# Attention scores by three fp32r passes instead of fp32, with a block diagonal for the leftover queries, in a fused attention and two-MLP kernel

## The chip, the cores and the metric

One core of a Trainium2 chip. The metric is device time in microseconds of one execution, lower is better.

## What is computed

Attention over 4 batches and 8 heads, 576 positions, head size 64, then two MLPs (512 to 2048 to 512) over the 2304 tokens, all to float32 accuracy. The part of the reference that matters:

```python
scores = scale * np.matmul(q, k.transpose(0, 1, 3, 2))        # scale = 1/8
thresh = np.max(scores, axis=-1, keepdims=True) - tau
scores = np.where(scores >= thresh, scores, -1000000000.0)
scores = scores - np.max(scores, axis=-1, keepdims=True)
attn = np.exp(scores)
attn = attn / (np.sum(attn, axis=-1, keepdims=True) + 1e-09)
return np.matmul(attn, v).astype(np.float32)
...
h = x @ w_in
g = np.maximum(h, 0.0) + alpha * np.minimum(h, 0.0)           # the second MLP: g = h - np.tanh(h)
return (g @ w_out).astype(np.float32)
```

The MLP weights come as float64.

## The kernel before, in words

Two heads stand side by side on the 128 partitions, head `h` on rows 0 to 63 and head `h + 1` on rows 64 to 127. A unit `u` is a pair of heads in one batch and one query block; there are 32. Block `qb = 0` has queries 0 to 255, `qb = 1` has 256 to 511 and brings the last 64 queries along as leftover. A unit is worked on in two visits of 128 queries (64 visits), and a unit with `qb = 1` in one leftover visit more (16). Two units of a batch in a row can have the same heads; then the second keeps the keys and values of the first (`brings`).

A visit (`attend`, L639) does: scores on TensorE in plain fp32 (L649), per head and per chunk of 320 and 256 keys, each head on its own row half, into the PSUM tiles `sc0` and `sc1`; the row maximum on VectorE (L523); threshold (L526); a steep Prelu on ScalarE that leaves zero above the threshold and something very low under it (helper L289); Exp with its sum (L533); then the softmax is scaled and turned. Units 0 to 3 (`WHOLE = 4`) turn it with TensorE (L551, L554) and multiply with plain fp32 values (L674, L677). The others split it into two fp16 parts in a buffer of the tag `rw` (L571 and its ScalarE copy at L284, L575, then a small copy at L286 or L284) and turn it with a transposing DMA (L585) into a tile `eT`; values are split into three bf16 parts (L502) and multiplied in 46 matmuls (L637). The result goes as a high and a low fp32r part into `x0`, `x1` (L284, L691), the input of the first MLP. The leftover visit (`attend_left`, L706) does the same for 64 queries of both heads at once: its scores are four 64x64 tiles (L715).

An MLP in fp32r takes three passes: high by high, high by low, low by high. The first products stand on L782 (12 matmuls of 256 columns per 128 features), the second ones of the first MLP on L969, those of the second MLP on L891 and L898. The first MLP has nine blocks of tokens; block 2b + qb needs the four units of that batch and query block, the ninth needs all leftovers. The second MLP starts after the last product of attention, block by block as the first MLP's blocks are stored. All weights are brought from float64 into two fp32r parts by ScalarE, VectorE and GpSimd (`turned_float`, L321, and `piece`).

Queries and keys have buffers of their own (tags `q` and `ks`, two each). Both are loaded by SP (L476, L484), and ScalarE multiplies the queries by 1/8 in place (L284, from L479).

The order of the work on every engine is laid out ahead by a planner (`Plan.order`, L114). Each operation has a cost for each engine that may do it, a rank, reads, writes, and the buffers it takes. The planner keeps a clock for each engine and always issues the operation that can start first, the lower rank winning among equals. Where several engines may do an operation, the one with the lowest start plus a penalty gets it (`POOL_PEN`, `ACT_PEN`, `DVE_PEN`). The ranks come from `TA` (per visit), `PA` and `PB` (weights), `MLP_PE`, `MLP_G`, `PREP` and the table `OFF`; the buffer counts from `BUFS`. TensorE fills its waits at the start with 220 small matmuls (`warm`, L1016). SP issues every DMA, and does so in order.

Of the kernel before, what the change touches and what calls it, by code (L numbers as in the profile page):

```python
# [52 lines left out]
POOL_PEN = 0.8491  # L53
ACT_PEN = 0.7974
# [6 lines left out]
XR = -5886.5085  # L61
# [3 lines left out]
DVE_PEN = 0.7259  # L65
OFF = {"S": -1656.89, "M": -1361.12, "TH": -2264.05, "E": -795.89, "X": -1209.11, "R": -3863.73, "N": -3770.75, "NL": -1862.72, "F": -1987.79, "DT": 37.37, "T": 495.28, "H": -576.12, "AV": -1213.3, "XC": -519.32, "XH": 818.59}
# [3 lines left out]
    "q": 2, "ks": 2, "vs": 4, "v3": 3, "e": 3, "st": 2, "eT": 3, "rw": 4, "raw0": 2, "raw1": 3, "tw": 2,  # L70
# [161 lines left out]
def attention_mlp_mlp(ctx: ExitStack, tc: tile.TileContext, kv, q0, q1, tau, w1i, w1o, alpha, w2i, w2o, out):  # L232
# [23 lines left out]
    none = cpool.tile([P, P], F32, name="none")  # L256
    ident = tpool.tile([P, P], F32, name="ident")
# [200 lines left out]
    brings_v = [brings[u] if u != WHOLE else u for u in range(NV // 2)]  # L458
# [6 lines left out]
    def prep(u, rank):  # L465
        b, qb, h = visits[2 * u]
        k = brings[u]
        q, ks = ("q", u), ("ks", k)
        width = BLK + D * qb
        rate = P * 4 / DMA_RATE  # L470


        def load_q(e):
            x = take(tpool, q, [P, BLK + D], F32, "q", BUFS["q"])
# [6 lines left out]
        def load_k(e):  # L481
            x = take(tpool, ks, [P, S], F32, "ks", BUFS["ks"])
            for a in range(2):
                e.dma_start(out=x[HALVES[a]], in_=kv[b, h + a][HALVES[a], :S])  # L484

        add({"SYNC": max(1.1, rate * width)}, rank - 6, load_q, [ROOM], [q], takes=[("q", q)], lag=DMA_LAG)
        if k == u:
            add({"SYNC": max(1.1, rate * S)}, rank - 6, load_k, [ROOM], [ks], takes=[("ks", ks)], lag=DMA_LAG)
        add({"ACT": 0.45}, rank, scale, [("const", 0), ROOM], [q])
        k = brings_v[u]  # L490
# [21 lines left out]
    def softmax(tile, n, slots, rank, eT, alone=False, w=False):  # L512
# [125 lines left out]

    def attend(v, rank):  # L639
# [6 lines left out]
        def scores(e, heads):  # L646
            for c in CHUNKS:
                for a in heads:
                    e.matmul(  # L649
                        sc[slots[a]][:, 192:192 + S][:, c], lhsT=T["q", u][HALVES[a], j * P:(j + 1) * P], rhs=T["ks", k][HALVES[a], c],  # L650
                        start=True, stop=True,
                    )

        alone = v < SOLO
        for heads in ((0,), (1,)) if alone else ((0, 1),):
            add({"PE": 1.3}, rank + OFF["S"], lambda e, heads=heads: scores(e, heads), [("ks", k), ("q", u), ROOM], [("sc", slots[a], "s") for a in heads],
# [5 lines left out]
    def attended(u, rank):  # L662
        b, qb, h = visits[2 * u]
        k, w = brings_v[u], one(u)
# [16 lines left out]
        add({"PE": 2.3 if w else 2.7}, rank + OFF["AV"], products, [*reads, *with_v(k, w), ROOM], [pk, ("products", u)], bank)  # L681
# [323 lines left out]
    def clear(e):  # L1005
        e.memset(none, 0.0)
        make_identity(nc, ident)
# [127 lines left out]
```

## Time and profile before

| | |
|---|---|
| median of 3 runs | 1083.64 us (1081.25 to 1085.19) |
| profiled execution, its own time | 1083.33 us |
| its span, first to last instruction | 1081.5 us |
| TensorE busy | 1058.8 us, 98% |
| VectorE busy | 768.2 us, 71% |
| ScalarE busy | 569.5 us, 53% |
| GpSimd busy | 124.1 us, 11% |

The span is the time from the first to the last recorded instruction; the execution's own time holds a little more. Busy time of TensorE counts a matmul from its start to its modelled end, and matmuls overlap, so busy is not the same as working at full rate. In the rows, PE is TensorE's matmuls, PEld its weight loads, DVE is VectorE, ACT ScalarE, POOL GpSimd and SP the engine that issues DMAs.

### The profile page before, as it was taken

The page shows a single profiled execution, that of the slowest core. Times are in us where ns is not written, and L with a number is a line of the kernel's source. Part 1 is how long each engine was busy: PE and PEld are TensorE (multiplying, and loading weights), DVE is VectorE, ACT ScalarE, POOL GpSimd, SP SyncE. Part 2 cuts the span into 40 slices and gives each one's busy share as a digit, 9 for nine tenths or more (in the row PEclk, how much of TensorE's full clock was granted, in tenths as well). Part 3 has the DMA queues.
Part 4 walks back from the last instruction along what each step waited for, and adds up shares of the span by engine and source line. Part 5 has one row for each costly group of instructions (what it writes and reads, how often), then busy time and mean ns, then how long its engine had stood idle before and what let it go on. Part 6 is the DMA issues. An engine that isn't in the chain of part 4 may idle for free.

```text
span 1081.5 us, 23833 instructions
## 1 busy us (share of the span) xinstructions
PE 1058.8 (98%) x9594; PEld 979.0 (91%) x9594; DVE 768.2 (71%) x1638; ACT 569.5 (53%) x1135; POOL 124.1 (11%) x142
## 2 busy tenths in 40 slices
PE   9979999999999999999999999999999999999997
PEld 7658888888898888888899999999999999999997
DVE  6998978768778778777764558985656656556554
ACT  5777876766677677776642337642223322232322
POOL 2432211101111002120100001000000000000000
PEclk9989999999999999999999999999999999999999
DMA  8557987767566676756471315501101001010000
GB/s 228 178 156 185 226 172 127 142 112 145 110 148 135 111 148 144 147 126 132 84 214 44 118 58 197 177 25 35 41 1 40 19 21 40 2 40 21 1 21 20
DMA packets 189998, 110.55 MB, mean 102 GB/s; under 512 B 160704, under 2 KB 172224, under 8 KB 189888
## 3 DMA queue, kind: packets, MB, share of 16 engines
q1 hardware_dynamic: 189888, 109.03, 43.1%
q8 instruction: 75, 1.23, 0.5%
q14 instruction: 35, 0.29, 0.1%
HBM read 61.28 MB, written 9.96 MB: 66 GB/s over the span
## 4 chain that ended last, share of the span: by engine, by line
PE 53%; DVE 1%; ACT 0%; issue 0%; DVEq 0%; ACTq 0%
PE hp L782 17%; PE sc L891 13%; PE pt L782 10%; PE acc L969 8%; PE sc L898 5%; PE pt L637 1%; PE sc L649 0%; PE sc L715 0%; ACT e L289 0%; DVE rw L575 0%; DVE st L523 0%; DVE o L924 0%; ACT e L533 0%; DVE rw L571 0%; DVE st L526 0%
## 5 line engine op out<-in xcount | busy, mean ns | idle before, releaser
L782 PE MATMUL hp<-x,ihi 128*128 128x256 f32 x1728 | 323.8, 287 | 4.4 <-DVE st L539 2.2
L782 PEld LDWEIGHTS hp<-x,ihi 128*128 128x128 f32 x1728 | 270.4, 193 | 17.5 <-issue 10.7
L782 PE MATMUL hp<-x,ilo 128*128 128x256 f32 x864 | 245.2, 284 | 0.0
L969 PE MATMUL acc<-g,ohi 128*128 128x256 f32 x1152 | 215.7, 287 | 0.0
L969 PEld LDWEIGHTS acc<-g,ohi 128*128 128x128 f32 x1152 | 179.3, 192 | 10.0 <-issue 9.4
L782 PEld LDWEIGHTS hp<-x,ilo 128*128 128x128 f32 x864 | 166.7, 193 | 0.0
L969 PE MATMUL acc<-g,olo 128*128 128x256 f32 x576 | 162.9, 283 | 0.0
L891 PE MATMUL sc<-wp,g 128*128 128x256 f32 x1134 | 144.9, 283 | 0.0
L891 PEld LDWEIGHTS sc<-wp,g 128*128 128x128 f32 x1134 | 140.0, 192 | 0.0
L289 ACT ACTIVATE e<-sc,st 128x576 f32<-128x576 f32 x144 | 101.8, 737 | 26.4 <-DVE st L526 25.5
L533 ACT ACTIVATE e<-e,natau 128x576 f32<-128x576 f32 x144 | 110.5, 771 | 0.4
L523 DVE TENSOR_REDUCE st<-sc 128x1 f32<-128x576 f32 x144 | 105.2, 747 | 7.6 <-PE sc L715 6.8
L969 PEld LDWEIGHTS acc<-g,olo 128*128 128x128 f32 x576 | 110.5, 192 | 0.0
L803 DVE SCALAR_TENSOR_TENSOR mr<-mr,nalpha,hp 128x256 f32<-128x256 f32 x144 | 63.5, 475 | 62.2 <-ACT mr L796 62.1
L575 DVE SCALAR_TENSOR_TENSOR rw<-e,st,rw 128x576 f16<-128x576 f32 x128 | 104.2, 840 | 2.9 <-ACT rw L284 2.5
L782 PE MATMUL pt<-x,ihi 128*128 128x256 f32 x576 | 105.2, 283 | 0.0
L782 PEld LDWEIGHTS pt<-x,ihi 128*128 128x128 f32 x576 | 90.9, 192 | 1.3
L292 DVE TENSOR_TENSOR g<-mr,g 128x512 fp32r<-128x512 f32 (+1 forms) x134 | 85.7, 639 | 5.0 <-ACT g L284 3.6
L649 PE MATMUL sc<-ks,q 64*128 64x320 f32 (+1 forms) x512 | 82.3, 433 | 1.1 <-ACT e L289 0.7
L796 ACT ACTIVATE mr<-hp 128x512 f32<-128x512 f32 x72 | 42.7, 593 | 76.0 <-PE hp L782 73.4
L782 PE MATMUL pt<-x,ilo 128*128 128x256 f32 x288 | 81.5, 283 | 0.0
L637 PE MATMUL pt<-eT,vs 128*64 128x256 f16 (+1 forms) x1584 | 74.3, 246 | 3.8 <-DMA eT<-rw 3.6
(103 smaller groups left out, 1398.4 us busy)
## 6 DMA issues: line engine op xcount, KB each, us to landing
vs<-in_kv_dram SPq DMA_DIRECT2D x58, 160.0 KB, 2.9
rw<-in_w1i_dram SPq DMA_DIRECT2D x16, 512.0 KB, 5.5
rw<-in_w1o_dram SPq DMA_DIRECT2D x16, 512.0 KB, 4.8
rw<-in_w2i_dram SPq DMA_DIRECT2D x16, 512.0 KB, 4.7
rw<-in_w2o_dram SPq DMA_DIRECT2D x16, 512.0 KB, 4.2
ks<-in_kv_dram SPq DMA_DIRECT2D x56, 144.0 KB, 3.1
x1d<-o SPq DMA_DIRECT2D x18, 256.0 KB, 2.6
rw<-x1d SPq DMA_DIRECT2D x9, 512.0 KB, 3.7
```

Source lines behind the costliest of these rows:

```text
L289: e.activation(out=out_, in_=in_, func=AF.Prelu, alpha=alpha, **kw)
L292: e.tensor_tensor(out=out_, in0=in_, in1=hi.bitcast(F32), op=ALU.subtract)
L523: e.tensor_reduce(out=T[st][:, 0, j:j + 1], in_=x(s), axis=AX.X, op=ALU.max, negate=True)
L533: e.activation(out=w_, in_=w_, func=AF.Exp, bias=natau, scale=1.0, accum_out=T[st][:, 2, j:j + 1])
L575: e.scalar_tensor_tensor(out=x_[:, S + D:], in0=w_, scalar=r, in1=x_[:, :S], op0=ALU.mult, op1=ALU.subtract)
L637: e.matmul(po[HALVES[a]], lhsT=plane((k, a), part, c), rhs=eT(a, block), start=(i == 0), stop=(i == len(TERMS) - 1), skip_group_check=True)
L649: e.matmul(sc[slots[a]][:, 192:192 + S][:, c], lhsT=T["q", u][HALVES[a], j * P:(j + 1) * P], rhs=T["ks", k][HALVES[a], c], start=True, sto ...
L782: e.matmul(hq[:, k, :], lhsT=weight(l, "i", part, f // 4)[:, c, (f % 4) * P:(f % 4 + 1) * P], rhs=T[f"x{x}", m][:, c, :], start=(n0 + n == ...
L803: e.scalar_tensor_tensor(out=T[r][:, k, :], in0=T[r][:, k, :], scalar=nalpha[:, f0 + k:f0 + k + 1], in1=hq[:, k, :], op0=ALU.mult, op1=ALU ...
L891: e.matmul(out_, lhsT=x[:, a], rhs=y[:, b], start=(n == 0 and i == 0 and number in (1, 2, 5, 4)), stop=(n == NPAIR - 1 and i == 2), skip_g ...
L898: e.matmul(two_banks(3 - 2 * t), lhsT=x, rhs=y, start=False, stop=(n == NPAIR - 1 and k == 1 and i == 2), skip_group_check=True)
L969: e.matmul(acc[t][:, (c % 2) * BLK:(c % 2 + 1) * BLK], lhsT=w[:, c * P:(c + 1) * P], rhs=g[:, k, :], start=(f == 0 and n == 0 and c % 2 == ...
```

## The change

From unit 4 on (`NATIVE = 4`) queries and keys are split into a high fp32r part and a low one, and the scores are the sum of three fp32r passes: high by high, low by high, high by low. Queries and keys are loaded into one tile of the tag `rw` (four buffers, shared with the fp16 parts and with the raw weights), and the parts go to the tags `qh` and `kh`, two buffers each. The high part is a copy on ScalarE, VectorE or GpSimd, the low part a subtraction on VectorE or GpSimd. The leftover queries of both heads go into a 128x128 block diagonal `last`, cleared once at the start, so that the leftover scores are six matmuls over all 128 rows. Units 0 to 3 keep plain fp32 scores, read from the raw tile. Queries are no longer scaled: the 1/8 goes into the threshold and into Prelu. Unit 4 now brings keys of its own. `vs` goes from four buffers to three, `eT` from three to two. The planner's constants and some of its costs are new.

```diff
-TA = 3.0306
-PA, PB = 1607.411, 3.1322
-MLP_PE = 1522.9469
-MLP_G = -1792.0778
-PREP = 2618.4454
-WHOLE, SOLO = 4, 0
+TA = 19.6723
+PA, PB = 2239.503, 0.1787
+MLP_PE = 139.5993
+MLP_G = -1579.1484
+PREP = 2168.8771
+WHOLE, SOLO, NATIVE = 4, 0, 4
...
-    "q": 2, "ks": 2, "vs": 4, "v3": 3, "e": 3, "st": 2, "eT": 3, "rw": 4, "raw0": 2, "raw1": 3, "tw": 2,
+    "qk": 2, "qh": 2, "kh": 2, "vs": 3, "v3": 3, "e": 3, "st": 2, "eT": 2, "rw": 4, "raw0": 2, "raw1": 3, "tw": 2,
...
-        same = u and visits[2 * u][::2] == visits[2 * u - 1][::2]
+        same = u and u != WHOLE and visits[2 * u][::2] == visits[2 * u - 1][::2]
...
+        parts = [("qh", BLK, 0, BLK)] + ([("kh", S, BLK + D, S)] if k == u else [])
...
+        def load_qk(e):
+            x = take(apool, raw, [P, 1024], F32, "rw", BUFS["rw"])
             for a in range(2):
                 e.dma_start(out=x[HALVES[a], :width], in_=packed_q[qb][b, h + a][HALVES[a]])
-        def scale(e):
-            copy(e, T[q][:, :width], T[q][:, :width], scale=qscale)
+            for a in range(2) if k == u else ():
+                e.dma_start(out=x[HALVES[a], BLK + D:BLK + D + S], in_=kv[b, h + a][HALVES[a], :S])
+        def hi(e, name, size, at, n):
+            copy(e, take(tpool, (name, u), [P, 2, size], F32R, name, BUFS[name])[:, 0, :n], T[raw][:, at:at + n])
+        def lo(e, name, at, n):
+            sub(e, T[name, u][:, 1, :n], T[raw][:, at:at + n], T[name, u][:, 0, :n])
+        def left_hi(e, a):
+            copy(e, last[HALVES[a], 0, HALVES[a]], T[raw][HALVES[a], BLK:BLK + D])
+        def left_lo(e, a):
+            sub(e, last[HALVES[a], 1, HALVES[a]], T[raw][HALVES[a], BLK:BLK + D], last[HALVES[a], 0, HALVES[a]])
...
+        for x in parts if u >= NATIVE else ():
+            name, size, at, n = x
+            y = (name, u)
+            add(any_of(0.1 + n * 0.00082, 0.07 + n * 0.00052, 0.09 + n * 0.001), rank + OFF["KS"], lambda e, x=x: hi(e, *x), [raw, ROOM], [(*y, 0)], takes=[(name, y)])
+            add(either(0.065 + n * 0.00105, 0.1 + n * 0.00232), rank + OFF["KS"], lambda e, x=x: lo(e, x[0], *x[2:]), [raw, (*y, 0), ROOM], [(*y, 1)])
...
-            e.tensor_scalar(out=T[st][:, 1, a:b], in0=T[st][:, 0, a:b], scalar1=1.0, scalar2=atau, op0=ALU.mult, op1=ALU.add)
+            e.tensor_scalar(out=T[st][:, 1, a:b], in0=T[st][:, 0, a:b], scalar1=qscale, scalar2=atau, op0=ALU.mult, op1=ALU.add)
...
-            prelu(e, take(tpool, ("e", (tile, j)), [P, S], F32, "e", BUFS["e"]), x(s), STEEP, bias=T[st][:, 1, j:j + 1], scale=1.0)
+            prelu(e, take(tpool, ("e", (tile, j)), [P, S], F32, "e", BUFS["e"]), x(s), STEEP, bias=T[st][:, 1, j:j + 1], scale=qscale)
...
+    def multiply_last(e, u, to):
+        kh, kl = (T["kh", brings[u]][:, part] for part in range(2))
+        for c in CHUNKS:
+            for i, (part, y) in enumerate(((0, kh), (1, kh), (0, kl))):
+                e.matmul(to[:, c], lhsT=last[:, part], rhs=y[:, c], start=(i == 0), stop=(i == 2))
+
+    def multiply(e, u, to, s, heads):
+        if u < NATIVE:
+            terms = [(T["qk", u], T["qk", brings[u]][:, BLK + D:])]
+        else:
+            (qh, ql), (kh, kl) = ([x[:, part] for part in range(2)] for x in (T["qh", u], T["kh", brings[u]]))
+            terms = [(qh, kh), (ql, kh), (qh, kl)]
+        for c in CHUNKS:
+            for i, (x, y) in enumerate(terms):
+                for a in heads:
+                    e.matmul(to(a, c), lhsT=x[HALVES[a], s], rhs=y[HALVES[a], c], start=(i == 0), stop=(i == len(terms) - 1))
```

The rest of the diff is the wiring of these, the new values of `OFF` and of the penalties, and costs such as 2.8 for 2.7 (a unit's product) or 0.72 for 0.705 (four products of the MLP).

## Rows read from the trace of the kernel before

**Rows 1.** The span and the mean granted clock of the core.

```profile
core 0: 1081.5 us, clock 0.995
```

**Rows 2.** Busy us (instructions) by stage: PE, PEld, DVE, ACT, POOL; clock, DMA, GB/s.

```profile
60.00:100.00 40.00, 33.60 (x290) 27.66 (x291) 36.48 (x74) 29.42 (x63) 11.03 (x12) 0.87 0.63 152
...
100.00:547.00 447.00, 441.22 (x4601) 390.80 (x4601) 351.61 (x759) 314.50 (x678) 68.09 (x87) 1.00 0.70 140
547.00:690.00 143.00, 143.00 (x1256) 142.83 (x1255) 94.63 (x190) 60.80 (x105) 4.93 (x4) 1.00 0.43 134
690.00:1081.50 391.50, 385.89 (x3019) 376.49 (x3017) 237.37 (x510) 121.87 (x210) 17.50 (x7) 1.00 0.08 27
```

**Rows 3.** Waits of TensorE's matmuls, 100 to 547 us: total, times, longest; the first line.

```profile
PE pt L637 <- DMA eT<-rw: 3.6, 6, 0.9
```

**Rows 4.** The chain that ended last: start, us, what; one of many alike.

```profile
556.13 2.88 PE hp L782 x24
```

**Rows 5.** Timeline of TensorE around one score visit: start us, us, instruction, count.

```profile
299.37 0.28 PE L782 MATMUL hp<-x,ilo 128*128 128x256 f32 x1
299.58 1.24 PE L649 MATMUL sc<-ks,q 64*128 64x320 f32 x8
300.75 0.51 PE L782 MATMUL hp<-x,ihi 128*128 128x256 f32 x2
301.10 0.28 PE L782 MATMUL hp<-x,ilo 128*128 128x256 f32 x1
```

**Rows 6.** The instructions of line 649: ns min/median/max, first and last start.

```profile
L649 PE MATMUL sc<-ks,q x512: 376/429/899, 11.4 to 533.2; 64*128 64x320 f32 x86, 64*128 64x256 f32 x85
```

**Rows 7.** Timeline of TensorE at the start of the second MLP.

```profile
693.85 2.91 PE L898 MATMUL sc<-wp,g 128*128 128x512 f32 x12
696.60 0.40 PE L782 MATMUL pt<-x,ihi 128*128 128x256 f32 x2
```

**Rows 8.** Timeline of TensorE around one leftover visit.

```profile
220.53 1.19 PE L715 MATMUL sc<-ks,q 64*64 64x320 f32 x8
...
221.98 0.27 PE L782 MATMUL hp<-x,ilo 128*128 128x256 f32 x1
```

**Rows 9.** Groups by line and shape: busy us, mean ns; and line 284's scaling of queries.

```profile
L286 DVE TENSOR_SCALAR wp<-tw 128x256 fp32r<-128x256 f32 x1 | 0.3, 286 | 0.0
...
L286 DVE TENSOR_SCALAR g<-mr 128x512 fp32r<-128x512 f32 x57 | 24.5, 430 | 1.6
...
L292 DVE TENSOR_TENSOR wp<-tw,wp 128x256 fp32r<-128x256 f32 x6 | 2.5, 419 | 0.3 <-ACT wp L284 0.3
...
L292 DVE TENSOR_TENSOR g<-mr,g 128x512 fp32r<-128x512 f32 x80 | 55.6, 695 | 4.9 <-ACT g L284 3.6
...
L286 DVE TENSOR_SCALAR eT<-hp 64x128 f32<-64x128 f32 x15 | 4.2, 279 | 0.2
...
L284 ACT ACTIVATE q<-q,qscale x32: 491/534/577, 10.6 to 507.0; 128x256 f32<-128x256 f32 x16, 128x320 f32<-128x320 f32 x16
```

**Rows 10.** The tile eT's instructions and landings; then groups by line and shape.

```profile
L637 PE MATMUL pt<-eT,vs x1584: 189/272/300, 87.6 to 550.5; 128*64 128x256 f16 x133, 128*64 128x64 f16 x65
...
L585 SPq DMA_TRANSPOSE eT<-rw x128: 1242/1314/2477, 70.5 to 545.2; - x128
...
DMA to landing us min/median/max: 3.2/3.4/5.9
...
L637 PE MATMUL pt<-eT,vs 128*64 128x256 f16 x1008 | 62.1, 274 | 3.7 <-DMA eT<-rw 3.6
...
L637 PE MATMUL pt<-eT,vs 128*64 128x64 f16 x576 | 12.2, 197 | 0.0
...
L284 ACT ACTIVATE rw<-e,st 128x576 f16<-128x576 f32 x71 | 54.2, 773 | 31.7 <-DVE st L539 12.2 <-issue 7.1 <-ACT e L533 3.5
...
L575 DVE SCALAR_TENSOR_TENSOR rw<-e,st,rw 128x576 f16<-128x576 f32 x128 | 104.2, 840 | 2.9 <-ACT rw L284 2.5
...
L284 ACT ACTIVATE rw<-rw 128x64 f16<-128x64 f16 x102 | 25.3, 253 | 43.3 <-DVE rw L575 41.5 <-DMA q<-in_q_dram 1.1 <-DMA ks<-in_kv_dram 0.4
```

More of the change, by code (lines that the diff above doesn't have):

```diff
@@ L481, in load_k @@
[L481 to L489, printed above, removed]
@@ L491, in prep @@
+        for a in range(2) if qb and u >= NATIVE else ():
+            y = ("last", a)
+            add(any_of(0.2, 0.12, 0.2), rank + OFF["KS"], lambda e, a=a: left_hi(e, a), [raw, ("const", 2), ROOM], [(*y, 0)])
+            add(either(0.14, 0.25), rank + OFF["KS"], lambda e, a=a: left_lo(e, a), [raw, (*y, 0), ROOM], [(*y, 1)])
+        k = brings[u]
         for a in range(2) if k == u else ():
@@ L637, in summed, with with_qk @@
                 e.matmul(po[HALVES[a]], lhsT=plane((k, a), part, c), rhs=eT(a, block), start=(i == 0), stop=(i == len(TERMS) - 1), skip_group_check=True)
+    def with_qk(u):
+        k = brings[u]
+        return [("qk", u), ("qk", k)] if u < NATIVE else [(name, x, part) for name, x in (("qh", u), ("kh", k)) for part in range(2)]
+    def multiply_last(e, u, to):
[13 more added lines that the diff above has]
+                    e.matmul(to(a, c), lhsT=x[HALVES[a], s], rhs=y[HALVES[a], c], start=(i == 0), stop=(i == len(terms) - 1))
     def attend(v, rank):
@@ L646, in scores @@
         def scores(e, heads):
[L647 to L652, printed above, removed]
+            multiply(e, u, lambda a, c: sc[slots[a]][:, 192:192 + S][:, c], slice(j * P, (j + 1) * P), heads)
         alone = v < SOLO
         for heads in ((0,), (1,)) if alone else ((0, 1),):
-            add({"PE": 1.3}, rank + OFF["S"], lambda e, heads=heads: scores(e, heads), [("ks", k), ("q", u), ROOM], [("sc", slots[a], "s") for a in heads],
+            add({"PE": 1.32 if u < NATIVE else 1.0}, rank + OFF["S"], lambda e, heads=heads: scores(e, heads), [*with_qk(u), ROOM], [("sc", slots[a], "s") for a in heads],
                 [b_ for a in heads for b_ in (("sc", slots[a], 0), ("sc", slots[a], 1))])
@@ L663, in attended @@
         b, qb, h = visits[2 * u]
-        k, w = brings_v[u], one(u)
+        k, w = brings[u], one(u)
         pk, po, bank = out_of(u)
@@ L707, in attend_left @@
         b, qb, h = visits[2 * u]
-        k, kv_ = brings[u], brings_v[u]
+        k = brings[u]
         s = u % 2
@@ L712, in scores @@
         def scores(e):
-            for c in CHUNKS:
-                for a in range(2):
-                    e.matmul(
-                        sc[s][HALVES[a], 192:192 + S][:, c], lhsT=T["q", u][HALVES[a], BLK:], rhs=T["ks", k][HALVES[a], c], start=True, stop=True,
-                    )
-        add({"PE": 1.3}, rank + OFF["S"], scores, [("ks", k), ("q", u), ROOM], [("sc", s, "s")], [("sc", s, c) for c in range(2)])
+            if u < NATIVE:
+                multiply(e, u, lambda a, c: sc[s][HALVES[a], 192:192 + S][:, c], slice(BLK, BLK + D), range(2))
+            else:
+                multiply_last(e, u, sc[s][:, 192:192 + S])
+        add({"PE": 0.8}, rank + OFF["S"], scores, [*(with_qk(u) if u < NATIVE else [("kh", k, 0), ("kh", k, 1), *[("last", a, part) for a in range(2) for part in range(2)]]), ROOM], [("sc", s, "s")], [("sc", s, c) for c in range(2)])
         softmax(-u - 1, 1, (s,), rank, [(eT_, 0, 1)])
@@ L1006, in clear @@
         e.memset(none, 0.0)
+        e.memset(last.bitcast(F32), 0.0)
         make_identity(nc, ident)
```

32 lines of the change are left out of this document (15 added, 17 removed).

## The prediction, made before the changed kernel was run

> **What bounds the kernel now.** I read the spans first, then the busy times by stage, then what TensorE waited for, then its order of work. The granted clock was 0.995 over a span of 1081.5 us [rows 1]; the profiled execution took 1083.33 us, so 1.8 us lie around the span, and it stands 0.3 us under the median of 1083.64. I make the sum against 1083.3. TensorE is busy for 441 of 447 us in the attention stage (100 to 547), for all of 547 to 690 and for 386 of 391 behind it [rows 2]. A busy TensorE can still be waiting, so I looked at its waits and its order. In the attention stage the largest thing it waited for comes to 3.6 us in all [rows 3], and in the dense stretches of the chain that ended last 24 matmuls of 256 columns take 2.88 us, 0.12 each [rows 4]. So from 100 us on the time is the sum of TensorE's work, and a pass less there is time less. Before that it is not: from 60 to 100 us VectorE is busy for 36.5 of 40, and TensorE has 6.4 us idle and a mean granted clock of 0.87 [rows 2]: part of it ran at 1.2 GHz instead of 2.4. That front belongs to VectorE.
>
> **Scores of the main visits.** One isolated visit: the last matmul of the MLP starts at 299.37, the third one after the scores at 301.10 [rows 5]. Three matmuls take 0.36, so the visit takes 1.37 us from the MLP. It falls apart so: 299.37 + 0.12 to 299.58 is 0.09 of emptying; the scores hold TensorE 1.17, until 300.75; and the first matmul behind is 0.35 instead of 0.24 ahead of the third, 0.11 for a weight load that nothing hides. I charge the scores the same two at their own ends (0.11 for the first load, 0.09 for the emptying): 1.17 - 0.20 leaves 0.97 for the passes. That both heads run at once shows in the instructions: eight, of 0.43 us in the median, lie in 1.17 [rows 5, 6].
>
> After the change a visit has 12 matmuls in six pairs, one pair per pass and chunk, on the same two row halves. The price of an fp32r pass is in the rows: 0.120 for 256 columns, and 12 of 512 take 2.75, from 693.85 to 696.60, so 0.229 each [rows 4, 7]. Between them lie 0.426 ns per column, so 320 columns cost 0.147. Passes: 3 x (0.147 + 0.120) = 0.80. The visit saves 0.97 - 0.80 = **0.17**. Visits 8 to 63 change, 56 of them: **9.5 us**. Bounds: no row shows fp32r in halves of 64 rows. If the halves ran one after the other the passes would be 1.60 (a loss of 0.63 a visit); if the load beside each pass cost nothing, the slope alone gives 3 x 576 x 0.426 ns = 0.74 (a gain of 0.23). I take 0.17, since the fp32 halves do run together.
>
> The Trainium skill has another price (TensorE: Matmul & The Clock Gate, Back-to-back issue gap): a lone warm matmul follows the one before after its columns at 2.4 GHz plus 2.5 ns. By it the passes would be 3 x (0.136 + 0.109) = 0.735 and the visit would save 0.235. The rows differ: 0.120 where it has 0.109.
>
> **Scores of the leftover rows.** Now they are four small tiles. The isolated one starts at 220.53 and the third MLP matmul behind at 221.98 [rows 8]: 1.45, less two steps of 0.12, with 0.09 of emptying ahead, is 1.30 taken. As a block diagonal they are six full matmuls, 0.80 by the same prices, and of the shape of the MLP's, so between MLP matmuls I expect neither emptying nor bare load: 0.50 saved. Where a product or a score visit stands on one side, one of the two stays; I take 0.45 as the mean. 16 x 0.45 = **7.2 us**; bounds 0.3 and 0.5, or 5 to 8.
>
> **The splits.** Each unit from the fifth on now needs a high part and a low part of its queries, and of its keys where it brings them. VectorE's prices [rows 9]: a copy of 256 columns 0.286, of 512 0.430, so 576 cost 0.47; a subtraction 0.419 and 0.695, so 0.76. Queries 0.71, keys 1.23; the four pieces of the block diagonal about 0.28 each (the 64x128 copy), 1.12. 28 x 0.71 + 25 x 1.23 + 16 x 1.12 = 69 us if all of it were VectorE's. (25, since units 12, 20 and 28 keep the keys of the unit before.) In the attention stage VectorE has 447 - 352 = 95 us idle, GpSimd is busy for 68 of 447, and ScalarE is rid of the scaling of queries, 32 x 0.53 = 17 us [rows 2, 9]. So from 100 us on I cost the splits at nothing; their cover is the early start of scores, and without it VectorE would stand at 94%. In the front there is no such room. Units 4 to 7 fall in it or right behind: 4 x (0.71 + 1.23 + 1.12) = 12.2 us. Bounds: 0, if ScalarE (which loses 4 scalings) and GpSimd take them, 12 if VectorE does, and a gain of up to 11.6 if the new order empties the front's 6.4 us of idle and the 5.2 us that a clock of 0.87 costs in 40 us. I take **3**, since GpSimd is busy for only 11 of 40 there [rows 2].
>
> **Edits with one answer.** The 1/8 in Prelu and in the threshold takes the place of a constant, in instructions that already read one number a row from memory: nothing, and if Prelu grew by it, ScalarE has 132 us idle in the attention stage [rows 2]. The first four units lose 4 x 0.5 us of ScalarE work in the front, where VectorE is later: nothing. Two more key loads (unit 4 brings its own) stand beside 56 and are issued a unit ahead: nothing. SP is an in-order queue: a load of queries and keys that waits for one of the four rw buffers holds the transposing DMAs behind it; this, two eT instead of three and three vs instead of four are the second rival below. The new ranks and costs move the order of every engine; the work they order is the same, and behind 690 us nothing else changes.
>
> Sum: 1083.3 - 9.5 - 7.2 + 3 = 1069.6, **1070**.
>
> **Rivals.** (1) *The front takes the splits in full.* For it: VectorE at 91% from 60 to 100 us. Against it: GpSimd's room. Then 1083.3 - 16.7 + 12.2 = 1079. (2) *The other side: attention becomes a loop through two eT and a shared rw.* The product of unit 4 starts at 87.6, the last ends at 551: 16.5 us a unit over 28 [rows 10]. Behind it lie 139 us of the first MLP up to 690; 2 x 384 matmuls (blocks 7 and 8, 92 us) must. So attention may end 47 us later, 1.7 us a unit, before TensorE runs dry; with 0.6 us less work a unit the point is 17.6 us. With two eT a unit's loop is four transposes at 1.31 with a landing of 3.4 (7.3), its product (62.1 / 28 for 36 of 46 matmuls, so 2.8), and for the leftover another 3.4 and a product of 1.0 (12.2 / 16, likewise) [rows 10]: 14.5, still under. If loads hold two rw buffers, the second visit's fp16 parts start only when the first's have landed: 2.1 for that, 0.77 + 0.84 + 0.25 for scaling, remainder and mending [rows 10], 4.0 in all. 18.5 is 0.9 over the point: 28 x 0.9 = 25, so 1070 + 25 = 1095. Against it: eT is late for TensorE in only 3.6 us now [rows 3], and qb = 0 units have no leftover. (3) *The halves run one after the other*: 56 x 0.63 = 35 lost, 1083.3 + 35.3 - 7.2 + 3 = 1114; the fp32 pairs speak against it. (4) *A pass costs its columns and no more*: by the slope of [rows 4, 7] alone 0.74 for the passes, so 56 x 0.23 + 16 x 0.51 = 21.0 saved, and 1065; for it speaks that the eight recorded fp32 matmuls fill 0.97 as four pairs over 2 x 576 columns, 0.84 ns a column or twice 0.42, with nothing on top; against it the 0.120. The page named above comes to about this time. (5) *The front gets shorter*: 1069.6 - 3 - 11.6 = 1055.
>
> **How the numbers follow.** Forecast 0.49 (its own range 1066 to 1075), columns alone 0.15, front in full 0.16, loop 0.13, halves in turn 0.04, shorter front 0.03. A measurement of this kernel tells about 0.3% from no change, 3.3 us. Faster: 0.49 + 0.15 + 0.03 and most of the front's case, 0.12, together 0.79. Same: the rest of the front's case and a loop just over its point, 0.04 + 0.04 = 0.08. Slower: 0.09 of the loop and the 0.04: 0.13. The range of 1058 to 1084 leaves out the shorter front, most of the loop and the halves in turn, under 0.2.
>
> **What would show it.** Right: the score visit's instructions hold TensorE for about 1.0 us instead of 1.17, the leftover's for 0.80 with no bare load behind it; TensorE stays busy between 100 and 690, and the first MLP ends some 14 us earlier; behind it 391 us as before. Wrong: pairs of a score visit that start 0.12 apart instead of together; waits of TensorE for eT or for a score's split in the attention stage; SP waiting on rw for tens of us; a stretch from 60 to 100 us with TensorE idle for well over 6.4.

## The result, and the profile after

The changed kernel takes **1090.95 us** (median of 4 runs, 1089.59 to 1091.86), the kernel before 1082.95 beside it: a ratio of **1.0072 [1.0049, 1.0094]**. It is slower by 8 us; 1070 was forecast, and the time lies outside the range of 1058 to 1084. The profiled execution took 1090.89 us.

The first fence has the span and clock of after and its busy times by stage (columns as in [rows 2]); the second has three of these stages for before.

```profile
core 0: 1089.1 us, clock 0.987
60.00:100.00 40.00, 35.76 (x325) 31.84 (x324) 36.90 (x74) 29.50 (x63) 9.11 (x8) 0.88 0.57 151
100.00:150.00 50.00, 38.61 (x397) 34.48 (x396) 44.65 (x98) 39.24 (x80) 4.92 (x4) 0.88 0.87 201
150.00:170.00 20.00, 18.13 (x160) 16.77 (x158) 16.95 (x37) 15.95 (x32) 2.62 (x3) 0.88 0.72 174
170.00:547.00 377.00, 372.08 (x4021) 351.00 (x4022) 291.56 (x633) 285.05 (x611) 51.31 (x66) 1.00 0.63 125
```

```profile
100.00:150.00 50.00, 48.17 (x525) 42.62 (x525) 45.63 (x98) 39.44 (x84) 13.10 (x14) 1.00 0.95 214
150.00:170.00 20.00, 19.96 (x193) 17.90 (x192) 16.47 (x35) 13.52 (x30) 3.15 (x4) 1.00 0.72 148
170.00:547.00 377.00, 373.10 (x3889) 330.27 (x3888) 289.52 (x628) 261.54 (x566) 51.84 (x69) 1.00 0.67 129
```

Between 100 and 150 us TensorE is idle for 11.4 us instead of 1.8, and its granted clock there fell from 1.00 to 0.88; in the whole front the clock stood at 1.2 GHz for 27 us instead of 10, 17 of them between 100 and 170 us, where it was none before (the trace's record of the granted clock). By 200 us the kernel before has done 640 matmuls of the first MLP, the changed one 562 (counted in the trace): 78 x 0.12 = 9.4 us behind. It has also done one main visit's scores and one product fewer, some 2 to 4 us more. So by the prices of before it is 12 to 14 us behind at 200 us. From 170 us on TensorE is as busy as before. The last matmul of the first MLP starts at 688.3 before and at 696.0 after, 7.7 us later; from there to the end of the span both take 393 us. So all of the loss arises ahead of the second MLP, and most of the idle time ahead of 170 us. Behind 200 us the changed kernel regains 4 to 6 us, of the 12.5 that its remaining 42 main and 12 leftover visits were forecast to save (an estimate from one trace of each kernel).

Attention also lasts longer. Its last products start at 598 us instead of 551 [rows 10], and the MLP's matmuls take the freed places, so that TensorE is hardly idle behind it. The products through `eT`, and the stage after 547 us, of after:

```profile
L650 PE MATMUL pt<-eT,vs x1584: 196/272/421, 87.5 to 597.8; 128*64 128x256 f16 x134, 128*64 128x64 f16 x64
547.00:690.00 143.00, 142.28 (x1373) 139.78 (x1370) 103.74 (x210) 86.67 (x163) 4.60 (x6) 1.00 0.54 148
```

What is late there is the first MLP's weights. This is line 331 (330 before), SP's loads of the second half of the weights, and the subtractions that make their low part: first and last start in us, before first, then after.

```profile
L330 SPq DMA_DIRECT2D rw<-in_w1o_dram x16: 328/374/1432, 11.4 to 145.0; - x16
L292 DVE TENSOR_TENSOR olo<-tw,ohi x11: 671/682/692, 26.9 to 152.9; 128x512 fp32r<-128x512 f32 x11
```

```profile
L331 SPq DMA_DIRECT2D rw<-in_w1o_dram x16: 328/335/573, 23.3 to 158.4; - x16
L293 DVE TENSOR_TENSOR olo<-tw,ohi x11: 673/685/693, 33.4 to 169.0; 128x512 fp32r<-128x512 f32 x11
```

The loads begin 12 us later and end 13 later, and the low part is ready 16 us later. The waits of after's TensorE between 100 and 170 us (us in all, times, longest) show who misses it:

```profile
PE pt L650 <- DMA eT<-rw: 2.8, 3, 1.1
PE hp L810 <- DVE ilo L293: 2.6, 3, 1.1
PE sc L671 <- ACT e L290: 2.5, 1, 2.5
PE hp L810 <- ACT ohi L285: 1.9, 1, 1.9
PE acc L997 <- POOL olo L293: 1.3, 1, 1.3
PE acc L997 <- DVE ohi L287: 1.1, 1, 1.1
```

Of 13 us of waits there (two of 0.6 and 0.2 are left out), 7.1 are for parts of the weights (`ihi`, `ilo`, `ohi`, `olo`).

A visit that nothing holds up does what was forecast. Here is TensorE's timeline around an isolated score visit (line 671) and an isolated leftover visit (line 660) of after.

```profile
299.62 0.28 PE L997 MATMUL acc<-g,olo 128*128 128x256 f32 x1
299.83 1.05 PE L671 MATMUL sc<-kh,qh 64*128 64x320 f32 x12
300.82 0.50 PE L997 MATMUL acc<-g,ohi 128*128 128x256 f32 x2
301.16 0.28 PE L997 MATMUL acc<-g,olo 128*128 128x256 f32 x1
...
295.94 0.28 PE L810 MATMUL hp<-x,ilo 128*128 128x256 f32 x1
296.06 0.96 PE L660 MATMUL sc<-kh,last 128*128 128x320 f32 x6
296.86 0.41 PE L810 MATMUL hp<-x,ihi 128*128 128x256 f32 x2
297.11 0.29 PE L810 MATMUL hp<-x,ilo 128*128 128x256 f32 x1
```

The score visit takes 301.16 - 299.62 - 0.36 = 1.18 us from the MLP, where [rows 5] gave 1.37: 0.19 saved. Its twelve matmuls hold TensorE for 0.99; less the 0.20 of emptying and bare load, 0.79 is left for the passes, against 0.80 forecast. The leftover's six begin one step of 0.12 after the MLP's matmul and are followed 0.80 later by the next: no emptying, no bare load. By the same reckoning it takes 297.11 - 295.94 - 0.36 = 0.81, and 1.31 before (the median of 13 isolated ones), 0.50 saved.

Not every visit is like these. Of the 16 leftover visits only 7 stand between matmuls of the MLP after the change, 13 before, and only three of the 7 take 0.80 or 0.81. Of the 46 main visits behind 170 us, 8 are held up inside, 3.6 us in all: the matmuls behind the first one come late, and where the trace names what they waited for, it is a Prelu (line 290). So from 170 us on a main visit holds TensorE for 1.07 us in the mean, against 1.18 before. The visit that is held up longest:

```profile
226.69 0.41 PE L671 MATMUL sc<-kh,qh 64*128 64x320 f32 x1
227.46 1.05 PE L671 MATMUL sc<-kh,qh 64*128 64x320 f32 x11 [0.36 <-ACT e L290]
```

One price is left that I had put at nothing. These are Prelu and the threshold (min/median/max ns), before and then after:

```profile
L289 ACT ACTIVATE e<-sc,st x144: 717/740/752, 15.0 to 541.4; 128x576 f32<-128x576 f32 x144
L526 DVE TENSOR_SCALAR st<-st,atau x80: 189/222/756, 14.7 to 540.5; 128x2 f32<-128x2 f32 x64, 128x1 f32<-128x1 f32 x16
```

```profile
L290 ACT ACTIVATE e<-sc,st,qscale 128x576 f32<-128x576 f32 x144 | 116.4, 826 | 42.3 <-DVE st L539 40.7 <-DVE st L552 0.9 <-DVE st L549 0.3
L539 DVE TENSOR_SCALAR st<-st,qscale,atau x80: 253/281/327, 10.2 to 582.0; 128x2 f32<-128x2 f32 x64, 128x1 f32<-128x1 f32 x16
```

With the scale read from memory a Prelu takes 826 ns instead of 737 (the mean of its group before) and a threshold some 60 more in the median. Both lie on each visit's way from its scores to its product.

### The profile page after: what moved, and what is told of

Read it like the earlier page. It is cut to its first block, busy times and chain, and to the rows that moved or that the text cites. A ratio compares the mean times of both kernels' runs of the same rounds, so it can differ in the third digit from the quotient of the medians.

```text
span 1089.1 us, 24301 instructions
## 1 busy us (share of the span) xinstructions
PE 1056.2 (97%) x9786; PEld 999.5 (92%) x9786; DVE 784.7 (72%) x1682; ACT 630.2 (58%) x1252; POOL 108.0 (10%) x120
## 4 chain that ended last, share of the span: by engine, by line
PE 72%; DVE 10%; DMA 8%; ACT 7%; issue 2%; SPq 1%; ACTq 0%; DVEq 0%
PE hp L810 23%; PE sc L919 12%; PE acc L997 12%; PE pt L810 10%; PE pt L650 6%; DMA eT<-rw 6%; PE sc L926 5%; PE sc L671 3%; DVE rw L588 3%; ACT e L290 3%; DVE st L536 2%; ACT e L546 2%; DMA rw<-in_w1i_dram 1%; ACT rw L285 1%; DVE mr L831 1%
## 5 line engine op out<-in xcount | busy, mean ns | idle before, releaser
L290 ACT ACTIVATE e<-sc,st,qscale 128x576 f32<-128x576 f32 x144 | 116.4, 826 | 42.3 <-DVE st L539 40.7
L588 DVE SCALAR_TENSOR_TENSOR rw<-e,st,rw 128x576 f16<-128x576 f32 x128 | 109.5, 865 | 26.5 <-ACT rw L285 25.7
L293 DVE TENSOR_TENSOR g<-mr,g 128x512 fp32r<-128x512 f32 (+1 forms) x141 | 90.7, 643 | 9.2 <-ACT g L285 7.7
L285 ACT ACTIVATE rw<-e,st 128x576 f16<-128x576 f32 x101 | 76.8, 769 | 31.9 <-DMA eT<-rw 20.7
L285 ACT ACTIVATE g<-mr 128x384 fp32r<-128x384 f32 (+1 forms) x109 | 62.9, 577 | 50.9 <-DVE mr L829 38.1
L650 PE MATMUL pt<-eT,vs 128*64 128x256 f16 (+1 forms) x1584 | 76.8, 249 | 6.2 <-DMA eT<-rw 6.2
```

The costliest lines, as they stand in the source:

```text
L285: e.activation(out=out_, in_=in_, func=AF.Copy, **({} if scale is None else {"scale": scale}))
L290: e.activation(out=out_, in_=in_, func=AF.Prelu, alpha=alpha, **kw)
L293: e.tensor_tensor(out=out_, in0=in_, in1=hi.bitcast(F32), op=ALU.subtract)
L588: e.scalar_tensor_tensor(out=x_[:, S + D:], in0=w_, scalar=r, in1=x_[:, :S], op0=ALU.mult, op1=ALU.subtract)
L650: e.matmul(po[HALVES[a]], lhsT=plane((k, a), part, c), rhs=eT(a, block), start=(i == 0), stop=(i == len(TERMS) - 1), skip_group_check=True)
```

## The experiments

Ratios are to the kernel before on the same chip, with 95% intervals; 0.001 is 1.08 us. A difference of two runs carries the intervals of both, some 1.5 to 3 us either way. All but the four of "orders searched anew" keep the written order of the kernel that they start from.

### Parts of the change taken out of the changed kernel

The theory was that the front pays for splits and that Prelu's scale lengthens the softmax chain; the rival, that the shared buffers and two `eT` make a loop. First the 1/8 as a constant:

```diff
-prelu(e, take(...), x(s), STEEP, bias=T[st][:, 1, j:j + 1], scale=qscale)
+prelu(e, take(...), x(s), STEEP, bias=T[st][:, 1, j:j + 1], scale=0.125)
```

(and `scalar1=0.125` in the threshold.)

> The changed kernel, in its own order, with the 1/8 as a constant in Prelu and in the threshold instead of a number per row from memory. Theory S (the scale from memory is what the order does not allow for: Prelu's mean went from 737 to 826 ns on the chain of each visit, 144 x 0.09 = 13 us of ScalarE): the time falls by 6 us or more, to 1085 or below, and Prelu's mean returns to 740 ns. Theory F (the front is starved by the splits and the buffers, Prelu is covered): within 2 us of 1091, though Prelu's mean returns to 740 ns.

1086.89 us, **1.0033 [1.0019, 1.0046]**: 4.2 us back, between what the two theories had expected. Its Prelu takes a median of 736 ns again. At 200 us it has done the same 562 matmuls of the first MLP, scores and products as the changed kernel: what it gains, it gains behind 200 us. Next, the main scores from unit 4 on as one plain fp32 pass over the high parts (the low parts are made and not used there):

```diff
-terms = [(qh, kh), (ql, kh), (qh, kl)]
+terms = [(qh.bitcast(F32), kh.bitcast(F32))]
```

> The changed kernel, in its own order, all splits kept, but the main visits from the fifth unit on take their scores in plain fp32 from the high parts alone (the low parts are made and not used, so the scores lack them). Both theories say that TensorE is the bound behind the front: a visit then takes 0.18 us more from the MLP, 56 of them 10 us, less what lies in the stretch up to 160 us where TensorE waits (some 14 visits, 2.5 us): 1098 to 1101. If the saved passes had gone nowhere, it stays within 2 us of 1091.

1095.25 us, 1.0109 [1.0092, 1.0126]: 4.0 us worse than the change, where 56 x 0.19 = 10.6 us of TensorE's work came back. That is less than the 1098 to 1101 expected. So the three passes do help, but bring some 4 us (about 3 either way) and not 10. Then without the low parts' subtractions (the low parts are left out, and every pass takes high by high):

```diff
-sub(e, T[name, u][:, 1, :n], T[raw][:, at:at + n], T[name, u][:, 0, :n])
+return
...
-terms = [(qh, kh), (ql, kh), (qh, kl)]
+terms = [(qh, kh), (qh, kh), (qh, kh)]
```

> The changed kernel, in its own order, without the subtractions that make the low parts (the three passes all multiply the high parts, so the scores lack the low ones). It takes 0.42 us of queries and 0.75 us of keys a unit and the leftover's 0.22 twice off VectorE or GpSimd, 12 of 28 units' worth on VectorE. Theory F: the front gets shorter, 4 us or more, to 1087 or below, and the first MLP's weights are ready earlier. Theory S: within 2 us of 1091.

1084.91 us, 1.0016 [1.0004, 1.0029]: 6.1 us back. "Nothing" for the splits is refuted. But the weights are hardly earlier: the last subtraction of line 293 on VectorE starts at 165.9 instead of 169.0. Both together:

> The changed kernel, in its own order, with both edits of the first call at once: the 1/8 as a constant, and no subtractions for the low parts (the scores lack the low parts). The first call gave 4.2 us for the one and 6.2 us for the other against the changed kernel's 1091. If the two costs lie on different stretches or chains, they add: 1080 to 1082, faster than the kernel before. If both are the same slack on one chain (VectorE's front), little is added: 1084 or more.

1083.11 us, **0.9997 [0.9987, 1.0006]**. It lies between the two forecasts. The scale and the low parts are worth 8.1 us together, as much as the whole loss. Without them the change is even with the kernel before, for all its shorter visits. But the front stays late without them. These are f1's stage from 100 to 170 us, its weights and its subtractions:

```profile
100.00:170.00 70.00, 57.84 (x609) 52.44 (x610) 58.98 (x126) 57.14 (x122) 8.32 (x7) 0.88 0.82 196
L331 SPq DMA_DIRECT2D rw<-in_w1o_dram x16: 327/334/571, 23.9 to 154.2; - x16
L293 DVE TENSOR_TENSOR olo<-tw,ohi x11: 673/686/693, 33.4 to 164.5; 128x512 fp32r<-128x512 f32 x11
```

TensorE is idle there for 12.2 us (13.3 with the whole change, 1.9 before) at the same clock of 0.88. At 200 us f1 has done 576 matmuls of the first MLP and one main visit fewer than the kernel before, 9 us behind; it ends the first MLP 1.1 us ahead. So it regains some 10 us behind the front, of the same 12.5 of which the changed kernel regained 4 to 6 (estimates from one trace each). More than half of what scale and low parts cost arises behind 200 us, and the greater part of the front's delay has another reason.

The same scale put into the kernel before (line 529's `scale=1.0` and line 526's `scalar1=1.0` become `qscale`, and line 479 copies queries without scaling them):

> The kernel before, in its own order, with the 1/8 moved into Prelu and the threshold as a number per row from memory; the queries are still copied in place, without a scale, so that the order and the work stay. Theory S: slower than the kernel before by 4 us or more, since each visit's Prelu takes 0.09 us more, twice, and the front is on ScalarE and VectorE. Theory F: within 2 us of the kernel before.

1089.19 us, **1.0054 [1.0037, 1.0070]**. This is Prelu in it:

```profile
L289 ACT ACTIVATE e<-sc,st,qscale x144: 808/827/846, 15.1 to 546.8; 128x576 f32<-128x576 f32 x144
```

144 x 0.09 = 13 us more of ScalarE, which is idle for 132 of 447 us in that stage, and still 5.8 us of time. The price of the scale from memory, in Prelu and threshold together, is shown from both sides.

### Does TensorE's clock in the front cost the time?

137 added matmuls of zeros fill the idle time that the planner foresees for TensorE between 85 and 165 us:

```diff
+for _ in range(int((t - done) / 0.12) if 85 < t < 165 else 0):
+    nc.tensor.matmul(sc[0][:, 768:1024], lhsT=none.bitcast(BF16)[:, :P], rhs=none.bitcast(BF16), start=True, stop=True)
```

> The changed kernel, in its own order, with some 130 small matmuls of zeros put on TensorE where the order leaves it idle between 85 and 165 us (into columns of a PSUM tile that nothing reads). Theory C (part of the loss is TensorE's clock at 1.2 GHz, granted for 27 us of the front against 10 in the kernel before, because TensorE idles there): the clock stays at 2.4 GHz between 100 and 165 us and the time falls by 3 us or more. If TensorE is not what that stretch waits for (theory F alone), the clock stays up and the time does not move by more than 1.5 us, or rises by what the fill delays.

1099.28 us, 1.0138 [1.0122, 1.0153], with a mean clock of 0.987 as without them. Neither theory's case came about: the clock stood at 1.2 GHz for 27 us again, so this doesn't tell what it costs; it does tell that matmuls written into the order at foreseen idle times delay what follows them.

### Buffers and the early start, with orders searched anew

In these four the planner's constants were searched again by its own costs, so the order of every engine differs and a ratio is of limited force; they are read for the waits. With fp32r from unit 8 instead of 4 (`NATIVE = 8`; all but h3 also have the constant scale):

> The changed kernel with the 1/8 as a constant and with fp32r scores only from the ninth unit on (units 4 to 7 keep plain fp32 and need no splits), so that the 12 us of splits of these units leave the front; the order's constants were searched anew for it. It gives back some 3 us of TensorE's savings (8 visits x 0.18, 4 leftovers x 0.45). Theory F (the front, not TensorE, is where the splits of the first units cost): it beats the changed kernel with the constant alone (1086.9) by 4 us or more, to 1083 or below. If the front is late for another reason (order or buffers), 1086 or above.

1088.19 us, 1.0048 [1.0034, 1.0063]. Its weights are early again:

```profile
L331 SPq DMA_DIRECT2D rw<-in_w1o_dram x16: 327/334/1211, 22.0 to 142.9; - x16
```

From 100 to 150 us TensorE is busy for 46.5 and the clock is 1.00; from 150 to 170 it is idle for 4.8 and the clock is 0.83. So weights this early are possible with the new scores from unit 8 on. Since the whole order is new, it isn't shown that it is the splits of units 4 to 7 that push them back; f1 and e3, which drop the low parts and keep the order, speak against the low parts. The time didn't come out better. Three `eT` and one `kh`:

> The changed kernel with the 1/8 as a constant, three eT buffers again and one of split keys instead of two (the same memory), constants searched anew. Theory B (two eT hold up SP, which then brings weights late): SP's wait for the product at the transposes falls from 100 us to under 30, and the time falls to 1083 or below. If eT is not what the front waits for: SP's wait falls, and the time stays at 1085 to 1089.

1088.42 us, 1.0047 [1.0033, 1.0061]. The queue of SP had waited for a product to free an `eT` far longer after the change than before; before, then after, from 100 to 547 us:

```profile
SPq L585 <- PE pt L637: 15.5, 8, 4.1
```

```profile
SPq L598 <- PE pt L650: 76.1, 24, 5.6
```

Over the whole span the second is 99.7. In h2 it is 9.4 over the span, and the time is no better than e1's. So the loop through two `eT` is there, but taking it away brought nothing in this order and with one `kh`. The converse, the kernel before with two `eT` and three `vs`:

> The kernel before with two eT and three vs, as in the changed kernel, and nothing else of it; constants searched anew. Theory B: 3 us or more slower than the kernel before, with SP waiting for the product at the transposes for 50 us or more instead of 16. Otherwise within 2 us.

1088.26 us, 1.0041 [1.0027, 1.0055], the same wait of SP 110 us over the span: as theory B expected, against h2. Buffers or order: this run can't part them. And h1 and h2 in one:

> Both at once: the 1/8 as a constant, fp32r scores from the ninth unit on, three eT, one buffer of split keys, constants searched anew. If theories F and B both hold, it is the fastest of these, 1080 or below. If only F holds, within 2 us of the run with fp32r from the ninth unit on.

1090.94 us, 1.0085 [1.0066, 1.0103]: no sum of two gains.

### Doses of VectorE's and TensorE's work

On the kernel before, three row maxima into a scrap tile, which nothing reads, were added to each of units 4 to 7 (i1) or 8 to 31 (i2) at the first main visit:

```diff
+    scrap = cpool.tile([P, 1], F32, name="scrap")
...
+            if j == 0 and 4 <= u < 8:
+                for _ in range(3):
+                    nc.vector.tensor_reduce(out=scrap, in_=T["ks", k], axis=AX.X, op=ALU.max)
```

> The kernel before, in its own order, with three row maxima over the 576 keys (into a scrap column) put on VectorE at the first visit's scores of units 4 to 7 alone: some 2 us a unit, 8 us in all, about what the splits of these units cost. Theory F (up to some 170 us the kernel goes at the pace of VectorE, behind it at TensorE's): 4 to 8 us slower than the kernel before. If VectorE has room there: within 2 us.

> The same three row maxima, but at the 24 units from 8 to 31: 48 us of VectorE work behind the front. Theory F: within 2 us of the kernel before, for six times the work. If splits cost anywhere in the attention stage: 5 us slower or more.

1076.36 us, 0.9944 [0.9927, 0.9962], and 1102.82 us, 1.0189 [1.0168, 1.0211]. The first can't be the dose's doing: it adds work and is faster. Its gain lies in the second MLP too (387 us instead of 393), where nothing was added; the solution is the last group of runs. By the base found there (j1, 0.9893) the doses cost (0.9944 - 0.9893) x 1083 = 5.5 us and 32 us. The added instructions of i1 and of i2, by number and ns:

```profile
L656 DVE TENSOR_REDUCE scrap<-ks x12: 740/753/753, 57.4 to 129.5; 128x1 f32<-128x576 f32 x12
```

```profile
L656 DVE TENSOR_REDUCE scrap<-ks x72: 733/753/755, 148.2 to 550.9; 128x1 f32<-128x576 f32 x72
```

9.0 us cost 5.5 (3 either way) and 54 us cost 32: **some 0.6 us for each us of VectorE's work, in the front and behind it**, with VectorE 77% busy between 170 and 547. This is the price of three instructions in a row, put ahead of a visit's own row maximum in a written order; splits that a planner spreads may cost less. Next, less TensorE: the second chunk of scores is left out in 48 visits of units 8 to 31.

```diff
-            for c in CHUNKS:
+            for c in CHUNKS[:1] if u >= 8 else CHUNKS:
```

> The kernel before, in its own order, with the second chunk of scores (256 of 576 keys) left out in the 48 main visits of units 8 to 31 (stale scores stand there). TensorE loses 0.42 us a visit, 20 us in all. If the time behind the front is the sum of TensorE's work: 17 to 20 us faster than the kernel before, 1063 to 1066. If a good part of what TensorE saves there turns into waiting: 12 us or less.

1075.40 us, 0.9928 [0.9912, 0.9945]. An isolated visit takes 0.93 instead of 1.36, so 48 x 0.43 = 20.6 us of TensorE's work are gone, and 7.8 us of time. The same window of i3:

```profile
170.00:547.00 377.00, 363.00 (x3801) 319.90 (x3800) 289.16 (x625) 259.15 (x564) 53.62 (x69) 1.00 0.66 132
```

TensorE's 99% of before becomes 96%: it is idle for 10.1 us more, so about half of the time that was freed turned into waits. The longest of them, from 100 to 547 us, are for the turned softmax and for Prelu (3.6 and 0.6 us in the kernel before):

```profile
PE pt L637 <- DMA eT<-rw: 7.7, 14, 1.1
PE sc L715 <- ACT e L289: 4.7, 5, 2.3
```

The order of every engine stayed as written; how much a newly planned order would get back was not tried. The last dose is the block diagonal alone, in plain fp32, on the kernel before (GpSimd copies the queries into it):

```diff
-                for a in range(2):
-                    e.matmul(
-                        sc[s][HALVES[a], 192:192 + S][:, c], lhsT=T["q", u][HALVES[a], BLK:], rhs=T["ks", k][HALVES[a], c], start=True, stop=True,
-                    )
+                e.matmul(sc[s][:, 192:192 + S][:, c], lhsT=none, rhs=T["ks", k][:, c], start=True, stop=True)
```

> The kernel before, in its own order, with one part of the change alone: the leftover queries of both heads as a 128x128 block diagonal, but in plain fp32 and with no splits (GpSimd makes two 64x64 copies a unit at its second visit's scores, 32 in all). A leftover visit then takes about 1.0 us from the MLP instead of 1.30, 16 times, some 13 of them behind the front: 3 to 5 us faster than the kernel before, 1078 to 1080. If GpSimd's copies come late for TensorE, or the saving turns into waiting: within 2 us.

1082.28 us, 1.0001 [0.9989, 1.0013]: nothing, though its isolated leftover visits take 0.97 instead of 1.31 in the median, 16 x 0.34 = 5.4 us less. Whether the added copies or the chain took it back wasn't told apart.

### Where the tiles lie

What i1 and i2 share is the scrap tile. It lies in the pool of small constants and moves every tile of the working pools up by 32 bytes. So the tile was added alone; no instruction differs:

```diff
+    scrap = cpool.tile([P, 1], F32, name="scrap")
```

> The kernel before with one unused tile of 4 bytes in the pool of the small constants, which moves every tile of the working pools up by 32 bytes; no instruction differs. If the place of the moving tiles sets the step of the MLP's matmuls (116 to 118 ns instead of 120, as in i1_more_front and i2_more_rest), both MLP stages get about 6 us shorter each: ratio 0.989, second MLP 382 us long instead of 388, and the 8 us of row maxima in i1_more_front cost about 5 us after all. If those steps came from the added work in some other way, 1.000 and steps of 120 ns.

**1070.92 us, 0.9893 [0.9871, 0.9914].** The changed kernel with the same tile:

> The changed kernel with the same unused tile. If the place sets the step and the change's loss lies elsewhere, it gains as much as the kernel before does from the same tile: 1.0072 less 0.011, so a ratio of about 0.996, and the distance to j1_before_32 stays at 7 to 8 us. If the place was part of the change's loss, the distance shrinks below 4 us. If the place does nothing, 1.007.

1078.97 us, 0.9970 [0.9956, 0.9984]: 8.05 us above j1. The change loses the same at both places. With the tile in the first pool instead, so that the weights' matrices move by 32 bytes too:

> The kernel before with the unused tile in the first pool instead, so that the matrices of the weights in that pool move by 32 bytes too. If the distance of the moving tile to the weights counts, nothing is gained in the first MLP: 120 ns and a ratio of about 1.000. If the moving tile's own place counts, 116 to 118 ns and 0.989, as in j1_before_32.

1083.60 us, 1.0005 [0.9991, 1.0019]. And with a tile of 64 bytes (`[P, 16]`) in the pool of constants:

> The kernel before with an unused tile of 64 bytes in the pool of the small constants: the working pools move by 64 bytes. If it is the place within 64 bytes that counts, nothing changes: 120 ns and 1.000. If any move takes the tiles out of each other's way, 116 to 118 ns and 0.989.

**1069.64 us, 0.9882 [0.9862, 0.9901]**, the fastest of all, without a changed instruction. In the chain that ended last, one run of 24 matmuls of j1 and then one of j4, where [rows 4] has 2.88:

```profile
440.07 2.83 PE hp L783 x24
```

```profile
157.78 2.72 PE hp L783 x24
```

And the windows of the second MLP, with the number of matmuls done in 210 us, for before, j1, j3 and j4 in turn:

```profile
690.00:900.00 210.00, 210.00 (x1655) 205.58 (x1654) 134.68 (x291) 70.91 (x123) 10.00 (x4) 1.00 0.09 31
```

```profile
690.00:900.00 210.00, 210.00 (x1682) 205.60 (x1681) 133.98 (x284) 68.80 (x118) 12.50 (x5) 1.00 0.08 29
```

```profile
690.00:900.00 210.00, 210.00 (x1655) 205.59 (x1654) 134.73 (x290) 71.23 (x124) 10.00 (x4) 1.00 0.09 32
```

```profile
690.00:900.00 210.00, 210.00 (x1697) 205.58 (x1697) 135.49 (x289) 68.99 (x119) 12.50 (x5) 1.00 0.09 32
```

The step of 0.120, which I had taken for the price of 256 columns, belongs to one placement. The mean step of the first layer's matmuls within the second MLP, from the starts of the ones that follow each other there, is 0.1199 before, 0.1174 in j1 and j2, and 0.1167 in j4, with single steps down to 0.112. Move the weights along, and it is 0.120 again. Neither the place of the moving tiles alone sets it (j1 and j3 have the same), nor that of the weights alone (before and j1 have the same); before and j3 have the same distance between the two, and the same step.

j1 has a check of this inside. The first quarter of the second MLP's first-layer weights lies in the pool `epool`, which moves along with the moving tiles. Its matmuls keep the old step, 0.1190 to 0.1200 us in j1 by the mean of each 128 features (0.1164 to 0.1170 in the other three quarters). Two runs of 24 matmuls of j1's second MLP, the first with weights that stayed in place, the second with weights that moved along with the tokens:

```profile
789.75 2.80 PE hp L783 x24
800.32 2.87 PE hp L783 x24
```

## Why the prediction was wrong

- **The price of a visit: right where nothing holds it up.** For an isolated visit 0.17 and 0.50 were forecast, 0.19 and 0.50 came; the halves run together, so the third rival falls. But the sum took 0.17 for all 56 main visits, and those behind 170 us hold TensorE for only 0.11 less in the mean, since some wait inside. And 0.45 as the mean of the leftover visits counted on most of them standing between MLP matmuls; 7 of 16 do. The Trainium skill's price (TensorE: Matmul & The Clock Gate, Back-to-back issue gap) would have made the passes 0.735; they measure 0.79. The fast runs of 24 matmuls in j4, 2.72 or 0.113 each (the mean there is 0.117), come nearer to the page's 0.109 than to my 0.120: the price that I took from [rows 4] was one of a placement.
- **"From 100 us on the time is the sum of TensorE's work, and a pass less there is time less": this step failed first.** I took 441 busy us of 447 as proof. In the changed kernel TensorE is idle for 13.3 of the 70 us from 100 on. And behind the front a saving doesn't come back in full: i3 removed 20.6 us of that work and got 7.8 back, e2 put 10.6 back and cost 4.0, i4 got nothing for the leftover's own saving. TensorE with MLP work to spare between the visits shows as busy while the softmax chain holds visits up; with less work the waits show (i3). At the 0.38 of a us that each us returned in i3 and e2, the forecast's 16.7 were worth about 6.3. That share is no constant: the changed kernel regained 4 to 6 of 12.5 behind 200 us, f1, with a shorter softmax chain and less work on VectorE and GpSimd, some 10.
- **"I cost the splits at nothing": failed.** The splits came to 84 us by the groups of their lines, 31 on VectorE, 31 on GpSimd and 22 on ScalarE, against the 69 reckoned for VectorE alone. VectorE's idle 95 us were no full cover: three added instructions a unit cost some 0.6 us per us in i1 and i2. Taking the low parts out of the change gave 6.1 back (3.9 with the constant scale).
- **"The 1/8 in Prelu and in the threshold: nothing": failed.** 4.2 us in the change (all of it behind 200 us by e1's trace), 5.8 in the kernel before. The instructions did read one number a row already; a second one costs 89 ns. I had argued from ScalarE's idle time, as with VectorE. The Trainium skill has the price (ScalarE: Activation LUTs, What ACT_TABLE_LOAD costs: about 93 ns for each operand of one number a row), and the trace agrees; I hadn't looked there.
- **The front, +3, with a bound of 12, and the new order at nothing ("the work they order is the same"): too small.** By 200 us the changed kernel is 12 to 14 us of TensorE's work behind. From 100 to 170 us it is idle for 11.4 us more, and 17 us ran at half the clock, which is worth up to 8.5 us more (an estimate); it had been some 3.6 us ahead at 100. The first rival named the place, but priced only VectorE's own time; weights that come 16 us late were not in it. Without the low parts and the scale the weights still come 12 us late (f1). So of the front's loss the greater part is not the work of the low parts. How it divides among the new order, the buffers and the high parts stays open: f2 didn't move the clock, and h1 brought the loads back to their time under another order without a gain in the end.
- **The second rival (the loop through two `eT`): open.** SP's waits grew as it said, and attention took 18.2 us a unit ((598 - 87.5) / 28), near the rival's 18.5, and ended 47 us later. But TensorE's wait for `eT` from 100 to 547 us grew only from 3.6 to 5.3, it was idle for 0.7 us behind 547, and h2 took the loop away without a gain; h3, the kernel before with two `eT`, was 4.4 us slower, in another order.
- **Behind the first MLP nothing changes: right**, 393 us in both.

The account by runs, in us against the kernel before: the change +7.8; less 8.1 for scale and low parts is -0.3 (f1). In that stand the visits' gain and what the high parts' copies, the buffers and the order cost. By e2 and i4 the gain is 4.0 and the cost 3.7, but both were measured with other loads on the chain. By f1's own trace some 10 us regained behind the front stand against 9 lost in it. The parts of that cost were not told apart.

## What to carry to other kernels

An engine that is 99% busy need not set the pace of a stage, if it holds work that can fill any gap: before a saving is counted in full, remove some of that work and see what returns (here 0.38 of it, in the written order), and dose the engines that look idle (here some 0.6 of each added us came through). A constant operand that becomes a number per row was not free on the chain. And where most of the time is a matmul's step, try the place of the moving tiles against the weights first: one unused tile gave 1.1 to 1.2%, about what this whole change was forecast to bring.

## What the runs showed that was not expected

- The distance in memory between the moving tiles and the weights sets a matmul's step: 0.120 us at one, 0.117 in the mean at two others, 12 to 13 us over the kernel. The Trainium skill (SBUF — State Buffer, Who interferes with whom) has TensorE read the two through independent ports; in this kernel the step still depended on where the two lie against each other (j1 against j3, and within j1). By what path is not shown. Which distances are good was not mapped; two were tried, and both are better than the one at hand.
- A Prelu over 576 columns takes 737 ns with one number a row and 826 with two, in the mean; a threshold 222 and 281, in the median.
- The front's weights stayed late when the work that seemed to push them back was taken out in the same order (f1, e3): what looks like the cause of a delay has to be taken out before it is called one.
- An added dose of work can come out faster for a reason that has nothing to do with it. i1 would have "shown" that VectorE's time in the front is free, had its second MLP not been read.
